# Thirteen residual additions moved from VectorE to ScalarE and an adding DMA

## The chip, the cores and the metric

The kernel runs on one core of a Trainium2 chip. Five engines work side by side, each with its own queue that is served in order: TensorE (PE in the profile; PEld is its weight load), VectorE (DVE), ScalarE (ACT), GpSimd (POOL) and SyncE (SP), whose queue issues the DMAs of this kernel. The metric is the device time of one execution in microseconds.

## The reference

Two layers, each of a Fourier mixing block and a linear attention block, on x with 2048 rows and 640 columns:

```
x = x + Real(DFT_seq(DFT_hidden(layernorm(x))))      # block A
x = x + attention(layernorm(x)) @ wo                 # block B
x = x + Real(DFT_seq(DFT_hidden(layernorm(x))))      # block A
x = x + attention(layernorm(x)) @ wo                 # block B, the last pass is its second half
...
q, k, v = x @ wqkv, in 32 heads of 20
phi(t)  = where(t > 0, t + 1, exp(t)) + 1e-6
num = phi(q) @ (phi(k)^T v)          # per head
den = phi(q) . sum(phi(k)) + 1e-6
out = (num / den) @ wo
```

## The kernel before, in words

The rows of x lie in SBUF as 16 tiles of 128x640 (x0 to x15 in the profile), and stay there through all four blocks. Every matmul with weights is done as three products of rounded parts: a value is split into a high part (a cast, L180 on ScalarE) and a low part (the rest, L181, on VectorE or GpSimd), and the products high-high, high-low and low-high are summed in PSUM (`product`, L242).

The last pass is `outputs` of the second attention. It goes over the tiles n = 0 to 15. Ahead of tile n, several steps are made for later tiles:

- `weigh(m)` (L567): GpSimd multiplies the tile's phi(q) with the sums of phi(k), into a temporary (t) or a slot (s);
- `weighted(m)`: VectorE sums that over each head (L583, into den), adds 1e-6 (L584), takes the reciprocal (L585) and scales phi(q) with it (L587, L593);
- the scaled tile is transposed: for most tiles by TensorE into PSUM (L193); for the tiles in QTURNS (7, 9, 10, 11, 12, 13, 15) by a copy on ScalarE in another order (L661), a DMA out to memory and one back (`turn_out`, L201, and `turn_in`, L205; turn in the profile), and a transpose within blocks on VectorE (L210);
- the transposed tile is split into its high and its low part (L180, L181); the low parts of tiles 7 and 13 are GpSimd's (QLOWS), the others are VectorE's.

Then 30 pairs of matmuls make the product with the five combined weights (M, L242) in PSUM, VectorE adds it to x (the residual, L678), and SyncE's queue stores the tile to the output (L1325). A store goes out whole, or in two halves for the tiles in HALVES; tile 15 is multiplied, added and stored in halves.

Temporaries (t) come from a pool of 12 buffers, the PSUM tiles (ps) from one of 4. A scheduler of the language sets the order on VectorE, ScalarE, GpSimd and TensorE from its own estimate of times, and `k.ahead` moves single steps forward or back in it. SyncE's queue keeps the order of the code.

A check of the inputs (the lines from L1224 on) runs beside the work; its verdict, the flag, is read by every engine at the end of the pass.

Of the kernel before, what the change touches and what calls it, by code (L numbers as in the profile page):

```python
# [8 lines left out]
F32 = mybir.dt.float32  # L9
F32R = mybir.dt.float32r  # L10
AF = mybir.ActivationFunctionType
ALU = mybir.AluOpType
# [28 lines left out]
ANORM = ((1, 2, 4, 9, 13), (1, 2, 3, 5, 7, 8, 10, 12, 14))  # L41
QTURNS = (7, 9, 10, 11, 12, 13, 15)
QLEAD = 2
LULLS = (0, 0)
WLEAD = 4
WSLOTS = (7, 8, 9, 11, 12, 13)
VERDICT = 4
QLOWS = (5, 6, 7, 8, 13)
HALVES = (0, 1)
KEEP = (1, 2)  # L50
TOTAL = (3, 0)
EARLY = (14, 14)
# [13 lines left out]
class Spared:  # L66

    def __init__(self, k, pool):
        self.k, self.nc, self.pool = k, k.nc, pool
# [28 lines left out]
class K:  # L98
    def __init__(self, tc, ctx):
        self.tc, self.nc = tc, tc.nc  # L100
        nc = self.nc
        self.n = self.layer = self.part = 0
        self.general, self.ve = False, nc.vector
        self.cst = ctx.enter_context(tc.tile_pool(name="cst", bufs=1))
        self.psp = ctx.enter_context(tc.tile_pool(name="ps", bufs=4, space=bass.MemoryType.PSUM))
        self.ident = self.cst.tile([128, 128], F32, name="ident")
        make_identity(nc, self.ident)
        self.ones = self.cst.tile([128, 128], F32, name="ones")
        nc.vector.memset(self.ones, 1.0)
        self.mhalf = self.cst.tile([128, 1], F32, name="mhalf")  # L110
        nc.vector.memset(self.mhalf, -0.5)
        self.two = self.cst.tile([128, 2], F32, name="two")
        nc.vector.tensor_scalar(self.two, self.ident[:, 0 : 65 : 64], -1.0, 2.0, op0=ALU.mult, op1=ALU.add)

# [110 lines left out]
def halves(pu):  # L225
    return pu.rearrange("p (a b) -> p a b", a=2)[:, :, :HD]


def h2(t):
    return t.rearrange("p (a b) -> p a b", a=2)  # L230


def product(nc, pu, sh, sl, wh, wl, hs=range(2), cs=None):
    n, m = len(sh), sh[0].shape[1]
    for c in range(n) if cs is None else cs:
        for s, w, first, last in (
            (sh[c], wh[c], c == 0, False),
            (sh[c], wl[c], False, False),
            (sl[c], wh[c], False, c == n - 1),
        ):  # L240
            for h in hs:
                nc.tensor.matmul(  # L242
                    pu[:m, 512 * h : 512 * h + HD], s, w[:, HD * h : HD * h + HD], start=first, stop=last
                )


class Attention:
# [239 lines left out]
    def combine(self, G, late):  # L487
# [17 lines left out]
        with k.ahead("weigh", 0):  # L505
            qd = self.weighted(0, self.weigh(0))
            t1 = None if LULLS[k.layer] else self.weigh(1)
        late[0]()
# [3 lines left out]
        for js in ((NE - 1, NE - 2), range(NE - 2)):  # L512
# [8 lines left out]
            for j in js:  # L521
# [10 lines left out]
                kv[j] = hi, lo  # L532
        if LULLS[k.layer]:
            t1 = self.weigh(1, None, lull)
# [35 lines left out]
    def weighted(self, n, t1, ps=None):  # L570

        k, nc, pq = self.k, self.k.nc, self.PQ[self.order2[n]]
        heads = lambda t: t.rearrange("p (h d) -> p h d", d=DH)
        if ps is not None:
            den, rden = ps[:, :H], ps[:, H:]
        else:
            den, rden = (  # L580
                k.sm.tile([128, H], F32, tag="sm" + n, name=k.nm(n), bufs=2) for n in ("den", "rden")
            )
        nc.vector.tensor_reduce(den, heads(t1), axis=AX.X, op=ALU.add)  # L583
        k.ve.tensor_scalar(den, den, 1e-6, None, op0=ALU.add)  # L584
        nc.vector.reciprocal(rden, den)  # L585
        chunks = t1.rearrange("p (i c) -> p i c", i=ND)
        k.ve.tensor_tensor(  # L587
            chunks[:, :, :EC].rearrange("p i (h d) -> p i h d", d=DH),
            pq[:, : EC * ND].rearrange("p (i h d) -> p i h d", i=ND, d=DH),
            rden[:, : 6 * ND].rearrange("p (i h) -> p i h", i=ND).unsqueeze(3).to_broadcast([128, ND, 6, DH]),  # L590
            op=ALU.mult,
        )
        k.ve.tensor_tensor(  # L593
            chunks[:, :, EC:].rearrange("p i (h s) -> p h i s", h=2),
            pq[:, EC * ND :].rearrange("p (h i s) -> p h i s", h=2, i=ND),
            rden[:, 6 * ND :].unsqueeze(2).unsqueeze(3).to_broadcast([128, 2, ND, 4]),
            op=ALU.mult,
        )
        return t1
# [42 lines left out]
    def outputs(self, after, between=lambda n: None):  # L642

        k, nc, X = self.k, self.k.nc, self.X
        q = self.first
        wt, t1 = {1: self.next}, self.t1
        turns, lead = (QTURNS, WLEAD) if self.saved else ((), 3)
        early = lambda m: QLEAD if m in turns else 0
        for n, i in enumerate(self.order2):
            for m in range(n + 3, n + 1 + lead + QLEAD):  # L650
                if m < NT and m not in t1 and m not in wt and m - lead - early(m) <= n:
                    t1[m] = self.weigh(m, self.slot() if m in WSLOTS else None)
            if n + 1 < NT and n + 1 not in turns:
                tp = k.transposed(wt[n + 1])
            for m in range(n + 2, n + 3 + QLEAD):
                if m in t1 and m - 2 - early(m) <= n:
                    with k.ahead("weigh", m):
                        wt[m] = self.weighted(m, t1.pop(m))
                    if m in turns:
                        mixed = self.slot()  # L660
                        k.nc.scalar.copy(  # L661
                            mixed.rearrange("p (a b i) -> p b a i", a=4, b=ND),
                            wt[m].rearrange("p (b a i) -> p b a i", a=4, b=ND),
                        )
                        wt[m] = k.turn_in(k.turn_out(mixed), self.slot())
            pu = k.psum()
            parts = [range(2)] if n + 1 < NT else [(0,), (1,)]
            pus = [pu] + [k.psum() for _ in parts[1:]]
            for pu, hs in zip(pus, parts):
                product(nc, pu, *q, [m[0] for m in self.M], [m[1] for m in self.M], hs)  # L670
            between(n)
            if n + 1 < NT:
                with k.ahead("q", n):
                    q = k.turned(wt[n + 1], n + 1 in QLOWS) if n + 1 in turns else k.split_chunks(tp)
            for pu, hs in zip(pus, parts):
                of = lambda t: t[:, hs[0] : hs[-1] + 1, :]
                with k.ahead("res", n):
                    k.ve.tensor_tensor(of(h2(X[i])), of(h2(X[i])), of(halves(pu)), op=ALU.add)  # L678
                for h in [(x, x + 1) for x in hs] if n in HALVES and self.saved else [(hs[0], hs[-1] + 1)]:
                    after(i, *h)  # L680
# [848 lines left out]
```

## Time and profile before

| | us |
|---|---|
| median of 3 runs | 750.06 (749.22 to 750.5) |
| the profiled execution | 750.05 |
| its span | 748.1 |
| TensorE busy | 726.8 (97% of the span) |
| VectorE busy | 587.5 (79%) |
| ScalarE busy | 370.6 (50%) |
| GpSimd busy | 248.8 (33%) |
| chain that ended last: TensorE, VectorE, ScalarE | 80%, 11%, 5% |
| all DMA transfers | 98.79 MB on one hardware queue |

Times in the rows are microseconds from the start of the span, unless a column is in ns. A row of the chain of waits gives start, duration and what ran. A row of busy time by stage gives a window, and then the busy microseconds of each engine with its count of instructions. In a row of instructions the bracket at the end gives the idle time before, and what ended it.

### The profile page before, as it was taken

How to read it: one execution, taken by the hardware profiler on the slowest of the kernel's cores; microseconds unless marked ns; L12 is line 12 of the kernel's file. 1: busy time of each engine (PE TensorE's matmuls, PEld its weight loads, DVE VectorE, ACT ScalarE, POOL GpSimd, SP SyncE). 2: the span in 40 equal slices, each digit the busy share in tenths (PEclk: the TensorE clock that was granted, in tenths of full speed). 3: DMA queues.
4: the chain of work that ended last, by engine and by line, in shares of the span. 5: the costliest groups of instructions: out<-in, count | busy, mean ns of one | idle time of the engine just before them, and what ended most of it. 6: DMA issues, size and time to landing. Idle time of an engine off the chain costs nothing.

```text
span 748.1 us, 12729 instructions
## 1 busy us (share of the span) xinstructions
PE 726.8 (97%) x4734; PEld 690.4 (92%) x4734; DVE 587.5 (79%) x1156; ACT 370.6 (50%) x691; POOL 248.8 (33%) x281
## 2 busy tenths in 40 slices
PE   4999999999999999999999999999999999999998
PEld 1388999999999999899986999999999999989997
DVE  7997798768968785888984756966887886689983
ACT  7745655664345543455773336566532554441220
POOL 5237942120014002567773672026000020154300
PEclk9999999999999999999999999999999999999999
DMA  9332467345565840500043222644266435002553
GB/s 328 102 90 89 130 199 259 119 140 181 187 187 184 284 145 21 155 5 1 11 136 138 70 94 78 222 145 166 57 177 189 153 114 155 23 12 72 175 155 133
DMA packets 55549, 98.79 MB, mean 132 GB/s; under 512 B 5268, under 2 KB 22935, under 8 KB 55479
## 3 DMA queue, kind: packets, MB, share of 16 engines
q1 hardware_dynamic: 55479, 97.89, 41.2%
q8 instruction: 39, 0.64, 0.3%
q14 instruction: 31, 0.25, 0.1%
HBM read 75.84 MB, written 21.63 MB: 130 GB/s over the span
## 4 chain that ended last, share of the span: by engine, by line
PE 80%; DVE 11%; ACT 5%; issue 2%; DMA 1%; POOL 1%; SPq 0%; DVEq 0%; ACTq 0%
PE ps L242 49%; PE ps L335 18%; PE ps L1150 4%; PE ps L1096 4%; PE ps L517 2%; PE ps L193 1%; PE ps L1055 1%; DVE t L181 1%; DVE w L181 1%; ACT t L879 1%; DVE ps L583 1%; DVE x L609 1%; ACT t L880 1%; ACT ab L916 1%; DVE t L587 1%
## 5 line engine op out<-in xcount | busy, mean ns | idle before, releaser
L242 PE MATMUL ps<-w,t 128*128 128x320 f32 x2880 | 432.6, 310 | 0.5 <-DVE w L181 0.2
L242 PEld LDWEIGHTS ps<-w,t 128*128 128x128 f32 x2880 | 422.9, 188 | 2.2 <-DVE t L181 0.7
L335 PE MATMUL ps<-t,t 128*128 128x256 f32 (+1 forms) x640 | 139.9, 309 | 0.0
L1224 DVE CUSTOM_DVE_ANT_0 junk<-ck,ck 128x688 bf16<-128x688 f32 (+5 forms) x138 | 103.6, 751 | 6.4 <-DMA ck<-in_ck 4.7
L335 PEld LDWEIGHTS ps<-t,t 128*128 128x128 f32 x640 | 106.9, 188 | 0.0
L335 PE MATMUL ps<-w,t 128*128 128x384 f32 (+1 forms) x320 | 98.6, 310 | 0.6 <-DVE w L181 0.6
L367 ACT ACTIVATE t<-ps 128x640 f32<-128x640 f32 x64 | 45.1, 704 | 95.8 <-PE ps L242 95.7
L180 ACT CAST t<-t 128x640 fp32r<-128x640 f32 x62 | 45.2, 728 | 71.2 <-DVE t L210 41.1
L567 POOL TENSOR_TENSOR t<-pq,t 128x640 f32<-128x640 f32 x26 | 42.1, 1626 | 105.6 <-ACT t L485 76.9
L404 POOL TENSOR_TENSOR t<-t,s 128x640 f32<-128x640 f32 x16 | 28.7, 1792 | 129.4 <-DVE s L370 122.6
L335 PEld LDWEIGHTS ps<-w,t 128*128 128x128 f32 x320 | 60.2, 188 | 1.1 <-DVE w L181 0.9
L181 DVE TENSOR_TENSOR t<-t,t 128x640 fp32r<-128x640 f32 x52 | 43.3, 833 | 18.9 <-ACT t L180 11.1
L1096 PE MATMUL ps<-t,u 128*128 128x322 f32 x306 | 48.1, 315 | 1.3 <-DVE t L181 1.3
L1096 PEld LDWEIGHTS ps<-t,u 128*128 128x128 f32 x306 | 45.9, 189 | 2.5 <-issue 1.6
L369 ACT ACTIVATE t<-t 128x640 f32<-128x640 f32 x64 | 47.5, 742 | 0.0
L370 DVE SCALAR_TENSOR_TENSOR pq<-t,pq 128x640 f32<-128x640 f32 x32 | 27.7, 864 | 23.8 <-ACT t L369 23.8
L370 DVE SCALAR_TENSOR_TENSOR s<-t,s 128x640 f32<-128x640 f32 x32 | 26.9, 841 | 21.6 <-ACT t L369 21.4
L180 ACT CAST t<-ps 128x640 fp32r<-128x640 f32 (+1 forms) x36 | 24.9, 690 | 38.1 <-PE ps L193 34.9
L181 POOL TENSOR_TENSOR t<-t,t 128x640 fp32r<-128x640 f32 x10 | 16.3, 1634 | 74.5 <-ACT t L180 74.5
L180 ACT CAST t<-s 128x640 fp32r<-128x640 f32 x32 | 23.3, 728 | 29.7 <-DVE t L181 17.3
L1150 PE MATMUL ps<-cw,ab 128*128 128x512 f32 x80 | 35.6, 595 | 1.2 <-ACT ab L916 0.7
L181 DVE TENSOR_TENSOR t<-ps,t 128x640 fp32r<-128x640 f32 (+1 forms) x36 | 29.3, 815 | 8.2 <-ACT t L180 8.2
(196 smaller groups left out, 987.2 us busy)
## 6 DMA issues: line engine op xcount, KB each, us to landing
ck<-in_ck SPq DMA_DIRECT2D x48, 346.0 KB
ck<-in_ck SPq DMA_DIRECT2D x48, 344.0 KB
turn<-t SPq DMA_DIRECT2D x23, 320.0 KB
save<-w SPq DMA_DIRECT2D x20, 320.0 KB
w<-save SPq DMA_DIRECT2D x20, 320.0 KB
z<-turn SPq DMA_DIRECT2D x19, 320.0 KB
x<-in_x SPq DMA_DIRECT2D x16, 320.0 KB
out<-x SPq DMA_DIRECT2D x13, 320.0 KB
```

The lines of the kernel that those rows point to most:

```text
L180: self.nc.scalar.copy(hi, src)
L181: return self.engine(pool).tensor_tensor(lo, src, hi.bitcast(F32), op=ALU.subtract)
L242: nc.tensor.matmul(pu[:m, 512 * h : 512 * h + HD], s, w[:, HD * h : HD * h + HD], start=first, stop=last)
L335: nc.tensor.matmul(self.place(G, c, part), x[:, 128 * c : 128 * c + 128], p[:, f : f + n], start=start and i == 0, stop=stop and i == 2, s ...
L367: nc.scalar.activation(h2(e), halves(pu), AF.Relu, scale=-1.0)
L369: nc.scalar.activation(e, e, AF.Exp, scale=-1.0)
L370: k.ve.scalar_tensor_tensor(out, e, 1e-6, out, op0=ALU.add, op1=ALU.add)
L404: k.engine(n not in PKSUMS[k.layer]).tensor_tensor(pksum, pksum, pk, op=ALU.add)
L567: k.behind(k.nc.gpsimd.tensor_tensor(t1, self.PQ[self.order2[n]], self.zb, op=ALU.mult), lull)
L1096: self.k.nc.tensor.matmul(po[:, o : o + 322], s[:, f : f + 128], w[:, x, :], start=start, stop=stop)
L1150: self.k.nc.tensor.matmul(self.sum(j), T.out["o", q][:, 128 * j : 128 * j + 128], self.C[2, g], start=n == 0, stop=n == 3)
L1224: i = nc.vector.tensor_tensor_reduce(k.junk[:, : a.shape[1]], b, a, 1.0, 0.0, op0, op1, o)
```

## The change

For tiles 1 to 13 of the last pass, VectorE's residual is replaced: ScalarE copies the product from PSUM to a temporary y, and a DMA issued from GpSimd's queue adds y to the tile of x in SBUF. The tile is stored one step later (ALAG), and the store waits for that DMA. Tiles 0, 14 and 15 keep VectorE's residual. Tile 14 is now the one that is stored in halves, beside 0 and 15; tile 1 is stored whole. In the last pass the addition of 1e-6 to den of tiles 2 to 15 is an activation of ScalarE, whose constant is a new tile `tiny` that GpSimd fills at the start.

```
+ADDED = (1, 2, 3, 4, 5, 6, 7, 8, 9, 10, 11, 12, 13)
+ALAG = 1
+SHIFTED = tuple(range(2, 16))
-HALVES = (0, 1)
+HALVES = (0, 14)
...
+        self.tiny = self.cst.tile([128, 1], F32, name="tiny")
+        nc.gpsimd.memset(self.tiny, 1e-6)
...
-        k.ve.tensor_scalar(den, den, 1e-6, None, op0=ALU.add)
+        if k.part == 3 and n_ in SHIFTED and not k.general:
+            nc.scalar.activation(den, den, AF.Identity, bias=k.tiny)
+        else:
+            k.ve.tensor_scalar(den, den, 1e-6, None, op0=ALU.add)
...
+            if n - ALAG in landed:
+                after(landed.pop(n - ALAG), 0, 2)
+            if self.saved and n in ADDED:
+                y = k.temp()
+                with k.ahead("res", n):
+                    nc.scalar.copy(h2(y), halves(pu))
+                    nc.gpsimd.dma_start(X[i], y, accum_op=ALU.add)
+                landed[n] = i
+                continue
```

The scheduler sets the order anew around these instructions. Three places follow; the lines of the changed program stand higher by 5 to 17 (L567 is L572, L181 is L186, L201 and L205 are L206 and L210, L1325 is L1342), and buffer numbers differ.

GpSimd's queue, from the weighing of tile 5 (t_1314) to the low part of tile 7 (t_1372 before, t_1377 now). Before:

```order
L567 TENSOR_TENSOR t_1314_7573<-pq_1262_7287,t_1234_7216 128x640
L567 TENSOR_TENSOR t_1322_7628<-pq_1279_7386,t_1234_7216 128x640
L567 TENSOR_TENSOR t_1342_7747<-pq_972_5525,t_1234_7216 128x640
L567 TENSOR_TENSOR s_1341_7745<-pq_879_4979,t_1234_7216 128x640
L567 TENSOR_TENSOR s_1349_7814<-pq_900_5097,t_1234_7216 128x640
L567 TENSOR_TENSOR s_1360_7876<-pq_925_5226,t_1234_7216 128x640
L181 TENSOR_TENSOR t_1372_7941<-t_1370_7939,t_1371_7940 128x640
```

And now:

```order
L572 TENSOR_TENSOR t_1314_7575<-pq_1262_7289,t_1234_7218 128x640
L572 TENSOR_TENSOR t_1323_7630<-pq_1279_7388,t_1234_7218 128x640
L689 DMA x1_100<-t_1322_7627 128x640
L689 DMA x2_102<-t_1330_7681 128x640
L572 TENSOR_TENSOR s_1344_7751<-pq_879_4981,t_1234_7218 128x640
L572 TENSOR_TENSOR s_1353_7822<-pq_900_5099,t_1234_7218 128x640
L572 TENSOR_TENSOR t_1345_7753<-pq_972_5527,t_1234_7218 128x640
L689 DMA x3_104<-t_1343_7748 128x640
L689 DMA x4_106<-t_1352_7819 128x640
L572 TENSOR_TENSOR s_1365_7886<-pq_925_5228,t_1234_7218 128x640
L689 DMA x5_108<-t_1364_7883 128x640
L186 TENSOR_TENSOR t_1377_7951<-t_1375_7949,t_1376_7950 128x640
```

Five adding DMAs now stand between the weighings and ahead of tile 7's low part.

VectorE's queue, where the last weight split (w_1304) and the first dens of the pass (den_1309 of tile 2, den_1317 of tile 3) stand. Before:

```order
L583 TENSOR_REDUCE den_1309_7528<-t_1305_7516 128x32
L181 TENSOR_TENSOR w_1298_7485<-ps_1296_7477,w_1297_7484 120x640
L181 TENSOR_TENSOR w_1301_7498<-ps_1299_7490,w_1300_7497 120x640
L584 TENSOR_SCALAR den_1309_7528<-den_1309_7528 128x32
L583 TENSOR_REDUCE den_1317_7583<-t_1306_7518 128x32
L181 TENSOR_TENSOR w_1304_7511<-ps_1302_7503,w_1303_7510 120x640
```

And now:

```order
L588 TENSOR_REDUCE den_1309_7530<-t_1305_7518 128x32
L186 TENSOR_TENSOR w_1298_7487<-ps_1296_7479,w_1297_7486 120x640
L186 TENSOR_TENSOR w_1301_7500<-ps_1299_7492,w_1300_7499 120x640
L588 TENSOR_REDUCE den_1317_7585<-t_1306_7520 128x32
L186 TENSOR_TENSOR w_1304_7513<-ps_1302_7505,w_1303_7512 120x640
```

The addition of 1e-6 is gone from between them; the rest kept its order.

SyncE's queue at the end of the pass, from the turn of tile 15 on. Before:

```order
L1325 DMA out_0<-x9_114 128x640
L1325 DMA out_0<-x10_116 128x640
L201 DMA turn_1410_8161<-s_1409_8159 128x4x160
L205 DMA s_1411_8163<-turn_1410_8161 128x640
L1325 DMA out_0<-x11_118 128x640
L1325 DMA out_0<-x12_120 128x640
L1325 DMA out_0<-x13_122 128x640
L1325 DMA out_0<-x14_128 128x640
L1325 DMA out_0<-x15_130 128x320 x2
```

And now:

```order
L1342 DMA out_0<-x8_114 128x640
L1342 DMA out_0<-x9_116 128x640
L206 DMA turn_1420_8181<-s_1419_8179 128x4x160
L210 DMA s_1421_8183<-turn_1420_8181 128x640
L1342 DMA out_0<-x10_118 128x640
L1342 DMA out_0<-x11_120 128x640
L1342 DMA out_0<-x12_122 128x640
L1342 DMA out_0<-x13_124 128x640
L1342 DMA out_0<-x14_130 128x320 x2
L1342 DMA out_0<-x15_132 128x320 x2
```

Each store of an added tile moved behind the turn of one step later, so that the turn of tile 15 now stands behind the store of tile 9 and not of tile 10.

More of the change, by code (lines that the diff above doesn't have):

```diff
@@ L570, in weighted @@
     def weighted(self, n, t1, ps=None):
-        k, nc, pq = self.k, self.k.nc, self.PQ[self.order2[n]]
+        k, nc, pq, n_ = self.k, self.k.nc, self.PQ[self.order2[n]], n
         heads = lambda t: t.rearrange("p (h d) -> p h d", d=DH)
@@ L645, in outputs @@
         q = self.first
-        wt, t1 = {1: self.next}, self.t1
+        wt, t1, landed = {1: self.next}, self.t1, {}
         turns, lead = (QTURNS, WLEAD) if self.saved else ((), 3)
```

## The prediction

> **What bounds the kernel now.** I read the busy time by stage first, then the chain of waits over the last pass, then the groups of instructions of that pass, and last the rows of GpSimd and of the DMA queue. The busy time (engines in the order PE, PEld, DVE, ACT, POOL; then granted clock, DMA share, GB/s):
>
> ```profile
> span 748.1 us, 12729 instructions
> 660.00:680.00 20.00, 18.24 (x124) 16.88 (x123) 17.57 (x32) 8.28 (x13) 11.52 (x8) 1.00 0.11 28
> 680.00:700.00 20.00, 20.00 (x143) 19.92 (x142) 19.96 (x38) 4.63 (x8) 5.70 (x4) 1.00 0.35 117
> 700.00:720.00 20.00, 20.00 (x137) 19.55 (x136) 19.87 (x35) 5.39 (x8) 6.73 (x4) 1.00 0.51 167
> 720.00:735.00 15.00, 15.00 (x105) 14.99 (x104) 8.80 (x14) 2.78 (x4) 1.57 (x1) 1.00 0.55 173
> 735.00:748.10 13.10, 9.41 (x65) 9.14 (x63) 4.65 (x6) 0.73 (x1) 0.00 (x0) 0.94 0.29 107
> ```
>
> From 680 to 720 us two engines are full at once: TensorE (40.0 of 40) and VectorE (39.8 of 40). Which of them sets the time is read from the chain:
>
> ```profile
> 667.43 0.72 DVE den L583
> 668.16 1.46 DVE w L181 x2
> 669.62 0.09 DVE den L584
> 669.71 0.72 DVE den L583
> 670.43 0.73 DVE w L181
> ...
> 673.12 0.83 PE ps L242 x4
> 673.95 0.55 PE ps L193 x5
> 674.50 4.39 PE ps L242 x30
> 678.88 0.55 PE ps L193 x5
> 679.43 4.39 PE ps L242 x30
> 683.82 0.55 PE ps L193 x5
> ...
> 688.77 0.55 PE ps L193 x5
> ...
> 693.73 0.55 PE ps L193 x5
> ...
> 698.67 0.11 PE ps L1245
> ...
> 703.99 26.68 PE ps L242 x180
> 730.66 0.55 PE ps L193 x5
> 731.21 13.21 PE ps L242 x90
> 744.42 0.02 issue
> 744.44 0.49 DVE x L678
> ```
>
> From 673.12 to 744.42 us every step of the chain is a matmul. A product of one tile (30 pairs, L242) takes 4.39 us, and six of them without a transpose between take 26.68 / 6 = 4.45. VectorE is full, but it is never late: nothing of it ends a wait of TensorE in these 71.3 us. So the 13 residuals that leave VectorE lie beside matmuls, and their time is not on the path.
>
> **The change part by part.** The groups of this pass from 673 us on (count | busy us, mean ns | idle time before):
>
> ```profile
> L678 DVE TENSOR_TENSOR x<-x,ps 128x640 f32<-128x640 f32 (+1 forms) x17 | 13.0, 770 | 6.5 <-PE ps L242 6.5
> L584 DVE TENSOR_SCALAR den<-den 128x32 f32<-128x32 f32 x12 | 4.7, 402 | 0.0
> L180 ACT CAST t<-ps 128x640 fp32r<-128x640 f32 x7 | 4.9, 694 | 19.2 <-PE ps L193 19.2
> L661 ACT COPY s<-s 128x640 f32<-128x640 f32 x5 | 3.6, 727 | 9.2 <-DVE s L593 9.2
> L181 DVE TENSOR_TENSOR t<-ps,t 128x640 fp32r<-128x640 f32 x7 | 5.7, 814 | 0.5 <-ACT t L180 0.5
> L567 POOL TENSOR_TENSOR t<-pq,t 128x640 f32<-128x640 f32 x4 | 6.3, 1570 | 10.9 <-issue 6.7 <-DVE t L593 4.2
> L181 POOL TENSOR_TENSOR t<-t,t 128x640 fp32r<-128x640 f32 x2 | 3.1, 1568 | 33.3 <-ACT t L180 33.3
> ```
>
> *VectorE* loses 13 x 0.77 = 10.0 us of residuals and 14 additions of 1e-6 (4.7 us for twelve), about 15 of 71 us. On the path this counts once: L584 stands for 0.09 us ahead of the last weight split (670.43), whose rows TensorE waits for at 673.12. Gain 0.09 us.
>
> *ScalarE* gains 13 copies out of PSUM; its nearest operation, the cast of the same shape from PSUM, takes 0.69, so 9.0 us, and 14 additions of 128x32 with no row of their own: between 0.1 (a short VectorE operation) and 0.69 each, taken as 0.2, so 2.8. It was busy 4.63 to 8.28 us in 20, so it has room. But its queue is in order: each copy waits for the end of a product, and the next tile's cast stands behind it. After the end of product n come the copy (0.69), mostly one reordering copy or addition (0.7), the cast (0.7) and VectorE's low part (0.8): 2.9 us, and the result is due 4.4 + 0.6 us after that end, when product n + 2 reaches its third pair. Spare 2.1 us, so nothing. VectorE's reciprocals now wait for ScalarE's additions behind the same copies; in the order they stand behind a low part that needs the same point of ScalarE's queue, so they take nothing more.
>
> *GpSimd* gains 13 DMA issues, each behind the copy of its tile, with weighing products (L567) and two low parts (L181) queued behind. The rows before:
>
> ```profile
> 680.54 5.16 POOL L567 TENSOR_TENSOR s<-pq,t 128x640 f32<-128x640 f32 x3
> 700.66 1.57 POOL L181 TENSOR_TENSOR t<-t,t 128x640 fp32r<-128x640 f32 x1 [14.96 <-ACT t L180]
> 702.18 2.09 POOL L567 TENSOR_TENSOR s<-pq,t 128x640 f32<-128x640 f32 x1
> 704.23 1.57 POOL L567 TENSOR_TENSOR t<-pq,t 128x640 f32<-128x640 f32 x1
> ```
>
> No row shows what such an issue holds GpSimd for; call it d. The nearest below is an issue of SyncE's queue, 0.34 us (row further down), the nearest above GpSimd's longest single operation here, 2.09. I take 1.6, its usual pass over 128 rows. Then: tile 1 from 679.6 (product end 678.88 + 0.7), tile 2 from 684.5 to 686.1, three weighings to 690.9, tile 3 to 692.5, tile 4 from 694.4 to 696.0, a weighing to 697.6, tile 5 from 699.4 to 701.0, and tile 7's low part from 701.0 to 702.6. Product 7 starts at 703.99 and wants it 0.6 us later: 2.0 us spare. Both ends of d cost nothing; with a larger d the issues queue up, and the low part ends at 692.5 + 4d, which passes 704.6 at d = 3.0. At tile 13 the sum is 726.9 + d + 1.6 against 731.8, d = 3.3.
>
> *The transfers.* Rows of the DMA queue, and of VectorE where it waited for one:
>
> ```profile
> 707.92 0.34 SPq L1325 DMA_DIRECT2D out<-x  x1
> 708.35 0.39 SPq L201 DMA_DIRECT2D turn<-s  x1
> ...
> 719.36 0.39 SPq L201 DMA_DIRECT2D turn<-s  x1
> 722.59 0.32 SPq L205 DMA_DIRECT2D s<-turn  x1
> ...
> 725.91 1.36 DVE L210 STREAM_TRANSPOSE t<-s 128x640 f32<-128x640 f32 x1 [1.55 <-DMA s<-turn]
> 738.73 6.56 SPq L1325 DMA_DIRECT2D out<-x  x4
> ```
>
> A plain 320 KB transfer takes 3.2 us from issue to landing (719.36 to 722.59). The adding one, from GpSimd's issue to landing (A), reads its destination too: from below 3.2, from above two transfers one after the other, 6.5. I take 4.5, nearer to the one, since from the row of 735 to 748.1 us the engines move 1.40 MB in 0.29 x 13.1 = 3.8 us, so a further pass of 320 KB is only 0.9.
> The page "DMA: Bandwidth & Descriptors" of the Trainium skill (Anatomy of one DMA) fits 2.0 us + bytes/436e3 to a transfer of GpSimd's queue; worked out as an estimate that is 2.75 us for 320 KB, and the sum would be the same by it, as it lies below every point at which A begins to cost.
>
> Who waits for A: SyncE's stores, and behind them the turning transfers of later tiles. Tile 13's turn stands behind the store of tile 7. Product 7 ends at 703.99 + 4.45 = 708.4; copy to 709.1, landing 713.6, turn out and in 6.5 more, 720.1, against 725.91 before, since the store of tile 8 no longer stands there. The others keep 5 us or more as well. Temporaries come free when an addition has landed; the tightest (ScalarE's copies of tiles 3 and 4, about 5 us after the landing of 1 and 2) allow A = 9. Cost 0. The DMA engines had 0.35 x 20 + 0.51 x 20 + 0.55 x 15 = 25.5 of 55 us busy from 680 to 735; eleven additions may take 2.7 us each before they are full, three plain passes.
>
> *The end.* Product 13 ends at 731.21 + 13.21 / 3 = 735.6, its copy at 736.3, the addition lands at 740.8, two microseconds later than its store went out before (738.73), and it is stored then; tile 14 in two issues follows by 741.6, tile 15's halves at 742.7 and 744.93 as before. SyncE's issues stand 0.43 us apart (707.92, 708.35), so the last is late only when tile 13 lands after 744.93 - 4 x 0.43 = 743.2, A = 6.9. Cost 0; for stores closer together at the end allow up to 0.3. The transpose of tile 14 moves by 28 matmuls into product 12 and stays the same 0.55 us.
>
> **Sum:** 0.09 gained, 0 to 0.3 lost at the end. The profiled execution took 750.05 us, its span 748.1 and 1.95 around it, and the median of the runs shown is 750.06. I forecast 749.9, no change that can be told: 0.2% is 1.5 us, about what a measurement of this kernel can tell.
>
> **The rivals.**
> *GpSimd's issue is long (slower).* Place: tile 7's low part behind the additions of 1 to 5; it decides from d = 3.0. At d = 4 the low part ends at 692.5 + 16 = 708.5, 3.9 us late: 754. Against it: 3.0 is above every single GpSimd operation of the pass. For it: VectorE and GpSimd hold each other up. L584 took 402 ns on average here but 0.09 in the chain, and the GpSimd product at 702.18 took 2.09 where its neighbour took 1.57. A VectorE operation that holds GpSimd out lasts up to 1.36 (the transpose at 725.91), so d = 1.6 + 1.36 = 2.96 if each issue meets one, and two such would make 4.3, 5.1 us late, 755.
> The Trainium skill's "SBUF — State Buffer" (A bandwidth-pool intuition) has the same trap: GpSimd cannot write its descriptors while VectorE uses the shared ports, and a transfer of 0.62 us took 3.1; by that figure as an estimate of d the low part would end at 704.9, 0.3 us late. The trace shows such blocking between operations, but no issue.
> *The additions are slow (slower).* If they take the DMA engines more than three passes, these are full and landings pile up; at the end each microsecond of A above 6.9 is one of time. A = 10 gives 750 + 3.1 = 753. Against it: A = 6.5 already charges two full transfers. For it: no adding transfer is in any row.
> *VectorE was the bound after all (faster).* If it were, 15 us less work would show. What is there to win is the wait in the first product (669 to 673.12, some 0.6 us beyond a product's 4.4) and 6 x 0.05 in the later ones: 749.1 at best, within 0.2%; for more the matmuls' spacing itself would have to shorten.
>
> **Chances.** No change that can be told 0.54; long issues 0.23 and slow additions 0.18, both slower by over 0.2%; faster by over 0.2% 0.05. Range: the forecast with its own bounds is 749.1 to 750.3, from which the low end is rounded down to 749.0; since the slower cases hold 0.41, it reaches to 755.5, past 753, 754 and 755, and leaves about 0.05 below and 0.13 above. Alone the likeliest case would have 749.0 to 750.6.
>
> **What would show it.** Right: TensorE's chain unbroken from 673 to 744, VectorE with some 15 us less from 680 to 735, GpSimd's low part of tile 7 done before 704, the store of tile 13 issued by 741. Wrong: a matmul (L242) that waits for GpSimd at product 7 or 13, SyncE's stores waiting over 5 us for an addition, DMA shares near 1, or the last store issued after 745.3. The forecast falls if d is above 3 us or A above 7.

## The result and the profile after

The changed kernel takes 752.65 us (median of 14 runs, 751.15 to 757.78) against 750.0 us of the kernel before beside it (14 runs); the medians differ by 2.65 us. The ratio, taken over all these runs, is 1.0041, 95% interval 1.0029 to 1.0052, or 3.1 us slower. The profiled execution of the changed kernel took 752.29 us, its span 750.2.

The busy time by stage of the changed kernel (PE, PEld, DVE, ACT, POOL; then granted clock, DMA share, GB/s):

```profile
span 750.2 us, 12769 instructions
660.00:680.00 20.00, 18.25 (x125) 17.49 (x125) 18.87 (x29) 9.56 (x18) 10.85 (x7) 1.00 0.11 27
680.00:700.00 20.00, 18.35 (x130) 18.01 (x129) 18.44 (x26) 7.49 (x15) 8.80 (x7) 1.00 0.67 165
700.00:720.00 20.00, 20.00 (x139) 19.79 (x139) 18.28 (x27) 9.52 (x17) 11.69 (x9) 1.00 0.85 214
720.00:735.00 15.00, 14.14 (x95) 13.48 (x94) 6.56 (x9) 4.76 (x8) 4.09 (x4) 1.00 0.90 225
```

TensorE, without a gap here before, loses 1.65 us between 680 and 700 and 0.86 between 720 and 735. The DMA share has gone from 0.35, 0.51 and 0.55 to 0.67, 0.85 and 0.90. TensorE's rows at the two gaps, with what ended each:

```profile
697.22 0.83 PE L247 MATMUL ps<-w,t 128*128 128x320 f32 x4
699.71 4.07 PE L247 MATMUL ps<-w,t 128*128 128x320 f32 x26 [1.65 <-DVE t L186]
...
727.61 4.89 PE L247 MATMUL ps<-w,t 128*128 128x320 f32 x30
733.36 12.85 PE L247 MATMUL ps<-w,t 128*128 128x320 f32 x86 [0.86 <-POOL t L186]
```

Product 6 waits after 4 of its 30 for VectorE's low part, and product 13 after 4 of its 30 for GpSimd's. Executions differ by a microsecond or two in what lies ahead of the last pass, so I measure from the start of the pass's first product (668.94 before, 667.59 now). To the start of product 7 it is 34.80 us before (668.94 to 703.74) and 36.74 now (667.59 to 704.33), 1.94 more. From there to the last matmul's end it is 40.66 (703.74 to 744.40) and 41.88 (704.33 to 746.21), 1.22 more. From there to the end of the span it is 3.70 and 3.99, 0.29 more. The sum is 3.45, and the runs show 3.1.

**The first gap.** GpSimd, VectorE and ScalarE of the changed kernel, in turn:

```profile
683.88 0.86 POOL L689 DMA_DIRECT2D x<-t  x1 [4.16 <-ACT t L688]
684.46 3.40 POOL L572 TENSOR_TENSOR s<-pq,t 128x640 f32<-128x640 f32 x2
687.51 1.86 POOL L572 TENSOR_TENSOR t<-pq,t 128x640 f32<-128x640 f32 x1
...
685.32 4.70 DVE L595 TENSOR_TENSOR s<-pq,rden 128x600 f32<-128x600 f32 x1
696.63 2.08 DVE L601 TENSOR_TENSOR t<-pq,rden 128x40 f32<-128x40 f32 x1
698.90 0.75 DVE L186 TENSOR_TENSOR t<-ps,t 128x640 fp32r<-128x640 f32 x1
...
690.22 0.73 ACT L669 COPY s<-s 128x640 f32<-128x640 f32 x1 [5.83 <-DVE s L601]
690.85 0.69 ACT L688 COPY t<-ps 128x640 f32<-128x640 f32 x1
691.44 0.69 ACT L185 CAST t<-ps 128x640 fp32r<-128x640 f32 x1
```

VectorE's scaling of phi(q) (L595), 0.71 to 0.78 us in this pass where GpSimd runs nothing beside it, lasts 4.70 us here: it starts inside the first of three weighing products that stand directly behind the adding DMA of tile 2, and ends 0.65 us after the last of them (689.37). A second operation of VectorE (L601, 0.19 without a GpSimd operation beside it) takes 2.08 at 696.63, behind the adding DMA of tile 4 and one weighing product (696.20 to 698.65). Behind the first, ScalarE's queue stands too: its reordering copy waits 5.83 us, and the copy of product 3 out of PSUM and the cast of tile 5 wait behind it, so that tile 5's low part starts at 692.17. Tile 6's low part is then the end of a backlog on VectorE: it is done at 699.65, and product 6, whose first four matmuls ended at 698.05, goes on at 699.71.

In the kernel before, four weighing products also ran in a row (679.02 to 685.70), but VectorE's rows there show no operation held for more than one of them:

```profile
679.93 1.30 DVE L587 TENSOR_TENSOR t<-pq,rden 128x600 f32<-128x600 f32 x1
681.16 1.56 DVE L593 TENSOR_TENSOR t<-pq,rden 128x40 f32<-128x40 f32 x1
684.10 1.64 DVE L584 TENSOR_SCALAR den<-den 128x32 f32<-128x32 f32 x2
```

**The second gap.** SyncE's queue of the changed kernel, with the turns of tiles 11, 12 and 13, and GpSimd's low part of tile 13:

```profile
706.76 0.39 SPq L206 DMA_DIRECT2D turn<-s  x1
713.84 0.32 SPq L210 DMA_DIRECT2D s<-turn  x1
...
714.73 0.40 SPq L206 DMA_DIRECT2D turn<-s  x1
720.06 0.33 SPq L210 DMA_DIRECT2D s<-turn  x1
720.44 1.04 SPq L1342 DMA_DIRECT2D out<-x  x1
721.57 0.52 SPq L206 DMA_DIRECT2D turn<-s  x1
726.02 0.32 SPq L210 DMA_DIRECT2D s<-turn  x1
...
731.73 1.58 POOL L186 TENSOR_TENSOR t<-t,t 128x640 fp32r<-128x640 f32 x1 [3.23 <-issue]
```

The turns out of tiles 11, 12 and 13 take 7.1, 5.3 and 4.4 us here (706.76 to 713.84, 714.73 to 720.06, 721.57 to 726.02), and all five from 701 on take 4.4 to 7.1; the seven of the kernel before took 2.6 to 3.4. SyncE waits for each before it issues the turn in, so tile 13's turn leaves at 721.57, and tile 13's low part is done 0.05 us before product 13 goes on at 733.36. The groups of the adding DMA, its queue over the whole kernel, and issue to landing (the last number of the last row):

```profile
L689 POOL DMA_DIRECT2D x<-t x13 | 11.5, 885 | 33.5 <-ACT t L688 30.0 <-ACT den L590 3.5
q0 software_dynamic: 1872, 4.26, 3.2%
x<-t POOLq DMA_DIRECT2D x13, 320.0 KB, 4.6
```

One adding DMA holds GpSimd 0.885 us, lands after 4.6 (median) and keeps all 16 DMA engines busy for 3.2% x 750.2 / 13 = 1.85 us.

### The profile page after: what moved, and what is told of

Its sections match the earlier page's. It is cut to its first block, busy times and chain, and to the rows that moved or that the text cites. A ratio compares the mean times of both kernels' runs of the same rounds, so it can differ in the third digit from the quotient of the medians.

```text
span 750.2 us, 12769 instructions
## 1 busy us (share of the span) xinstructions
PE 727.8 (97%) x4734; PEld 690.6 (92%) x4734; DVE 580.7 (77%) x1129; ACT 382.0 (51%) x718; POOL 259.7 (35%) x295
## 3 DMA queue, kind: packets, MB, share of 16 engines
q0 software_dynamic: 1872, 4.26, 3.2%
## 4 chain that ended last, share of the span: by engine, by line
PE 76%; DVE 10%; ACT 5%; DMA 4%; issue 2%; POOL 1%; SPq 1%; DVEq 0%; ACTq 0%
PE ps L247 42%; PE ps L340 18%; PE ps L1113 6%; PE ps L1167 4%; DMA turn<-s 3%; PE ps L1072 3%; DVE t L186 2%; PE ps L522 2%; DVE t L595 1%; PE ps L198 1%; DVE w L186 1%; ACT t L896 1%; DVE ps L588 1%; DVE x L617 1%; ACT t L897 1%
## 5 line engine op out<-in xcount | busy, mean ns | idle before, releaser
L572 POOL TENSOR_TENSOR t<-pq,t 128x640 f32<-128x640 f32 x26 | 43.8, 1692 | 100.4 <-ACT t L490 77.6
L186 DVE TENSOR_TENSOR t<-t,t 128x640 fp32r<-128x640 f32 x52 | 43.9, 844 | 22.1 <-ACT t L185 14.4
L186 DVE TENSOR_TENSOR t<-ps,t 128x640 fp32r<-128x640 f32 (+1 forms) x36 | 29.2, 811 | 10.5 <-ACT t L185 9.6
L160 POOL TENSOR_TENSOR kept<-ve,mhalf 128x1 f32<-128x1 f32 x32 | 21.7, 695 | 40.5 <-DVE ve L159 39.3
```

The lines of the kernel that those rows point to most:

```text
L186: return self.engine(pool).tensor_tensor(lo, src, hi.bitcast(F32), op=ALU.subtract)
L572: k.behind(k.nc.gpsimd.tensor_tensor(t1, self.PQ[self.order2[n]], self.zb, op=ALU.mult), lull)
```

## The experiments

Two theories first. H: GpSimd's weighing products, bunched behind the adding DMAs, hold VectorE out, and product 6 waits. L: the additions slow the turning transfers, and product 13 and the last store wait. Each kernel was timed in five rounds beside the kernel before (750.24 to 750.75 us there).

**One twentieth of the bytes.**

```
-                    nc.gpsimd.dma_start(X[i], y, accum_op=ALU.add)
+                    nc.gpsimd.dma_start(X[i][:, :32], y[:, :32], accum_op=ALU.add)
```

> Each adding DMA carries only the first 32 of 640 columns (the other 608 columns of these residuals are left out), so GpSimd's queue, the copies and all waits stay and the load on the DMA engines goes. Two theories of the 3.1 us: H, that GpSimd's weighings in a row behind the DMA of tile 2 hold VectorE out (one L595 of 4.70 us) and product 6 waits 1.65 us; L, that the additions load the DMA engines (1.8 us each), turns take 4.4 to 7.0 us instead of 3.2, and product 13 waits 1.3 us and the last store 0.3. Both: 751.7, product 6 still waits. H alone: 752.4. L alone: 750.0, and no wait at product 6.

Measured 752.34, ratio 1.0026 (1.0016 to 1.0036), 2.0 us. VectorE's held row and TensorE's rows of this kernel have the first gap whole and the second gone (the last row runs from product 12 to the end):

```profile
686.39 4.71 DVE L595 TENSOR_TENSOR s<-pq,rden 128x600 f32<-128x600 f32 x1
700.77 4.07 PE L247 MATMUL ps<-w,t 128*128 128x320 f32 x26 [1.66 <-DVE t L186]
728.68 17.26 PE L247 MATMUL ps<-w,t 128*128 128x320 f32 x116
```

So the first gap does not hang on the bytes that are added, and the second does; the 2.0 us that stay are about the first gap's 1.94. SyncE's stores wait for additions here as long as in the changed kernel (16.2 us in all from 674 to 730, against 15.9). The turns of tiles 10 and 11 take 2.7 and 3.5 us in place of 4.6 and 7.1, but those of tiles 12 and 13 still take 5.3 and 4.4.

**A plain DMA in place of the adding one.**

```
-                    nc.gpsimd.dma_start(X[i], y, accum_op=ALU.add)
+                    nc.gpsimd.dma_start(X[i], y)
```

> The same DMA without the addition (x of tiles 1 to 13 is overwritten by the product, the sum with x is left out); the order on every engine is the same. L: one pass instead of two, so 0.9 us of the DMA engines in place of 1.8 for each, turns of about 4 us, product 13 hardly waits: 751.7. H alone: 752.6, as the changed kernel.

Measured 751.37, ratio 1.0013 (1.0003 to 1.0023), 1.0 us. VectorE's L595 is held for 4.39 us and the L601 behind it for 1.76, 0.63 us less in all than in the changed kernel; product 6 waits 1.06, 0.59 less, and product 13 not at all. The same 4.26 MB take 1.5% of the span here, not 3.2%, in the row of the DMA queue:

```profile
q0 software_dynamic: 1040, 4.26, 1.5%
```

That is 1.5% x 749.3 / 13 = 0.86 us of all engines for each plain DMA, and an issue holds GpSimd 0.54 to 0.58 us (the first 0.82). Adding costs twice the transfer time and 0.3 us of GpSimd per issue.

**The first six tiles alone, the last seven alone.**

```
-ADDED = (1, 2, 3, 4, 5, 6, 7, 8, 9, 10, 11, 12, 13)
+ADDED = (1, 2, 3, 4, 5, 6)          # the one
+ADDED = (7, 8, 9, 10, 11, 12, 13)   # the other
```

> Only tiles 1 to 6 by the adding DMA, 7 to 13 by VectorE as before. H: the burst behind tile 2 stays, product 6 waits 1.65 us, nothing later: 751.7. L: the turns of tiles 11 to 15 come free again and nothing waits at product 13: with L alone 750.0.

> Only tiles 7 to 13 by the adding DMA, 1 to 6 by VectorE as before; GpSimd's weighings run early again. H: no long VectorE instruction and no wait at product 6, so 750.0 with H alone. L: the later turns are as slow as in the changed kernel, product 13 waits 1.3 us and the last store 0.3: 751.5.

Measured 753.29, ratio 1.0034 (1.0022 to 1.0047), 2.6 us, for the first six; 751.13, ratio 1.0007 (0.9998 to 1.0015), 0.5 us, for the last seven. With the first six, L595 is held 4.72 us, product 6 waits 1.68, and product 8 waits 0.89 more, behind a further VectorE operation, held 2.28 us by an issue and the weighing product behind it. H had priced the first six at less: it had left out the second place. With the last seven the DMA share from 720 to 735 us is the highest so far, and yet TensorE is without a gap there, in the busy time by stage:

```profile
720.00:735.00 15.00, 15.00 (x106) 15.00 (x105) 7.69 (x11) 4.98 (x8) 4.33 (x5) 1.00 0.97 254
```

So most of the loss comes from tiles 1 to 6, and load of the DMA engines as such does not make product 13 wait.

**Only the other half of the change**, the 1e-6 by ScalarE and tile 14 stored in halves.

```
-ADDED = (1, 2, 3, 4, 5, 6, 7, 8, 9, 10, 11, 12, 13)
+ADDED = ()
```

> Only the other half of the change: ScalarE adds the 1e-6, and tile 14 is the one that is taken in two halves; the residuals stay VectorE's additions out of PSUM and no adding DMA is issued. H and L both put the whole loss on the adding DMAs and the order round them: 750.0 to 750.3, the same as before, with no wait of TensorE between the products. Rival S (VectorE's reciprocals wait for ScalarE's additions of 0.32 us behind other work in ScalarE's queue, and this makes the low parts late): 751 to 752 with a wait of a product for VectorE's low part.

Measured 749.94, ratio 0.9995 (0.9985 to 1.0004): no change, and no wait of a product. The whole loss belongs to the adding DMAs and the order round them.

**Weighing products earlier, stores later, and both.**

```
-WLEAD = 4
+WLEAD = 6       # first and third kernel
-ALAG = 1
+ALAG = 2        # second and third kernel
```

> All 13 adding DMAs stay, but GpSimd's weighing products are written out two tiles earlier (WLEAD 6 for 4), so that most of them stand ahead of the first adding DMA instead of behind the first two. H (weighings held behind the issues come in a row and hold VectorE out): VectorE's chunk product (L595) no longer takes over 4 us near 685, product 6 does not wait for VectorE, and the time falls by 1.7 to 2 us to 750.8 to 751.2; what stays is product 13's wait of 1.3 us and the later last store. Rival (VectorE's low part of tile 6 is late for another reason, such as ScalarE's copies ahead of its cast): the wait of 1.65 us before product 6 stays and so does the time, 752.6.

> Each tile's store on SyncE's queue is written out one tile later (ALAG 2 for 1), so that it stands behind one more turning transfer and its addition has 4.4 us more to land. L as a matter of the queue (SyncE's stores stand waiting for additions and hold up the turning transfers behind them): tile 13's turn is issued several us before 721, product 13 does not wait, and 1.3 us come back: 751.5, the wait before product 6 as it is. L as a matter of load (the turning transfers themselves are slow because the adding ones share the DMA engines): the turns still take 4.4 to 7 us, product 13 still waits, 752.6. Either could lose up to 0.5 us at the end, where a store more is left behind the last product.

> Both repairs at once, all 13 adding DMAs kept: weighings two tiles earlier, stores one tile later. If H and the queue reading of L are the whole loss, both waits are gone and the time is 749.9 to 750.4, no different from the kernel before; if L is load, product 13's wait stays, 751.2. If it came below 749.5, the 15 us taken from VectorE would be worth something after all, which the unbroken TensorE chain of the kernel before speaks against.

Weighings earlier: 752.33, ratio 1.0031 (1.0019 to 1.0043), 2.3 us. Product 6 no longer waits, as H had it, but the time hardly falls. More weighing products now stand at the start of the pass, in a row up to 676.2, and hold VectorE there, one at a time (an L601 of 1.54 us at 672.67). The second product starts 6.07 us after the first (668.77 to 674.84; 5.31 before, 668.94 to 674.25), and product 13 still waits; TensorE's rows:

```profile
674.35 0.74 PE L198 MATMUL ps<-ident,t 128*128 128x128 f32 x5 [0.56 <-DVE t L601]
733.20 12.90 PE L247 MATMUL ps<-w,t 128*128 128x320 f32 x86 [0.77 <-POOL t L186]
```

Stores later: 754.87, ratio 1.0063 (1.0050 to 1.0077), 4.7 us. Product 13 no longer waits, as the queue reading had it; but the order on GpSimd moved by one weighing product, a further L595 is held (1.67 us, 693.77), and product 6 waits 2.83 us in place of 1.65. Both: 750.75, ratio 1.0008 (0.9999 to 1.0017), 0.6 us; no product waits after the second. Of the kernel with both, the turn of tile 13 on SyncE's queue, and the busy time of the two stages round it:

```profile
715.01 0.38 SPq L206 DMA_DIRECT2D turn<-s  x1
721.09 0.33 SPq L210 DMA_DIRECT2D s<-turn  x1
700.00:720.00 20.00, 20.00 (x139) 19.79 (x139) 13.34 (x24) 8.71 (x15) 8.96 (x8) 1.00 0.91 230
720.00:735.00 15.00, 15.00 (x105) 15.00 (x104) 5.52 (x6) 3.93 (x6) 4.18 (x4) 1.00 0.95 252
```

The DMA engines are fuller than in the changed kernel (0.91 and 0.95 against 0.85 and 0.90) and the turn takes 6.1 us, longer than there. But it starts 46.2 us after the first product (668.81 to 715.01), where it started 54.0 after it (667.59 to 721.57). So product 13's wait needs both: slow turns, and stores ahead of them in SyncE's queue that wait for additions. In the changed kernel these are the stores of tiles 1 to 4, ahead of the turns of 7, 9 and 10; from 701 to the turn of tile 13 none waits for one, and the queue moves on only as turns land. That the additions slow the turns is shown for tiles 10 and 11 alone; what makes those of 12 and 13 slow in the kernel with 32 columns too, these runs do not separate.

**One issue, and the same without an issue.** All holds of VectorE through more than one product so far stood directly behind a DMA issue of GpSimd; where four products ran in a row without one, in the kernel before, with the last seven and with the other half alone, VectorE got its turn. Theory G makes that the cause. Both kernels have the residuals on VectorE; STRAY is (1,), and the added statements are shown on lines of their own.

```
+        self.stray = self.cst.tile([128, 32], F32, name="stray")
...
                     k.ve.tensor_tensor(of(h2(X[i])), of(h2(X[i])), of(halves(pu)), op=ALU.add)
+                    self.saved and n in STRAY and nc.gpsimd.dma_start(k.stray, X[i][:, :32])      # the one
+                    self.saved and n in STRAY and nc.gpsimd.tensor_copy(k.stray, X[i][:, :32])    # the other
```

> No adding DMA at all: the residuals stay VectorE's additions (as with the moved 1e-6 alone), but behind tile 1's residual stands one plain 128x32 DMA of GpSimd's queue (16 KB, from x to a tile that nobody reads), so that four weighing products stand directly behind one issue that waited for tile 1, near 684. Theory G (behind a DMA issue GpSimd's operations run one after the other and VectorE's chunk product gets no turn between them): one VectorE operation on two SBUF operands (L595 or L601) lasts over 4 us there, and a product some 15 us later may wait 1 to 2 us: 751 to 752. Rival B (it is the late, dense run of weighings as such, and VectorE gets its turn after each): no VectorE operation lasts over 2.2 us, 750.0 to 750.5.

> The same kernel with GpSimd copying the 128x32 itself in place of the DMA issue: same wait for tile 1's residual, same four weighing products behind it, no issue. G: VectorE gets a turn after each weighing product, no VectorE operation on two SBUF operands lasts over 2.2 us, 750.0 to 750.5. If holding the weighing products back and running them close together is enough (B's opposite: any operation of GpSimd ahead of them does it), one lasts over 4 us as behind the issue and the time is that of the kernel with the issue.

With the issue: 757.22, ratio 1.0093 (1.0078 to 1.0109), 7.0 us for one transfer of 16 KB. Its rows of GpSimd, VectorE and TensorE:

```profile
680.85 0.82 POOL L695 DMA_DIRECT2D stray<-x  x1 [5.92 <-DVE x L695]
681.70 1.58 POOL L572 TENSOR_TENSOR t<-pq,t 128x640 f32<-128x640 f32 x1
683.22 4.52 POOL L572 TENSOR_TENSOR s<-pq,t 128x640 f32<-128x640 f32 x3
681.15 6.65 DVE L601 TENSOR_TENSOR t<-pq,rden 128x40 f32<-128x40 f32 x1
689.32 6.70 PE L247 MATMUL ps<-w,t 128*128 128x320 f32 x26 [4.56 <-DVE t L186]
```

Without it: 751.11, ratio 1.0010 (1.0001 to 1.0019), 0.75 us, of which a wait of 0.47 stands before one product for VectorE's late residual. VectorE's queue has the same order; the rows of GpSimd and VectorE:

```profile
680.12 0.69 POOL L695 COPY stray<-x 128x32 f32<-128x32 f32 x1 [5.68 <-DVE x L695]
680.78 1.58 POOL L572 TENSOR_TENSOR t<-pq,t 128x640 f32<-128x640 f32 x1
682.31 5.16 POOL L572 TENSOR_TENSOR s<-pq,t 128x640 f32<-128x640 f32 x3
682.72 1.79 DVE L595 TENSOR_TENSOR s<-pq,rden 128x600 f32<-128x600 f32 x1
684.43 1.56 DVE L601 TENSOR_TENSOR s<-pq,rden 128x40 f32<-128x40 f32 x1
```

G holds. Behind the issue an operation of 0.19 us lasted 6.65, from the issue through all four weighing products, which ran without a gap (6.0 us for four). Behind the copy the last three took 5.16 us, 0.64 more than behind the issue, because VectorE had its turns in between. G had priced the issue at 1 to 2 us, at a product some 15 us later; VectorE was held through all four products, product 3 waited for it right there, and TensorE was slow after the wait (below).

**Tiles 3 to 13 alone, stores one tile later.**

```
-ADDED = (1, 2, 3, 4, 5, 6, 7, 8, 9, 10, 11, 12, 13)
+ADDED = (3, 4, 5, 6, 7, 8, 9, 10, 11, 12, 13)
-ALAG = 1
+ALAG = 2
```

> The adding DMA for tiles 3 to 13 alone, each store one tile later. GpSimd's weighing products are then not held by tiles 1 and 2 (no wait of product 6), and SyncE's turns do not stand behind the additions (no wait of product 13). H and the queue reading of L: TensorE unbroken from the second product on, 750.3 to 750.8, of which 0.3 is the later end. If the loss came with every adding DMA alike (eleven of thirteen stay), 752.2. If G alone counts: two weighing products stand behind tile 3's issue, near 693, hold VectorE for 2.9 us there and cost a product up to 1 us: 751.5.

Measured 752.87, ratio 1.0031 (1.0019 to 1.0043), 2.3 us. All readings missed the place. Products 6 and 13 do not wait for a low part. But three weighing products now stand behind the issue of tile 3 (691.98 to 696.88), VectorE has nothing to do until the first is there (1.62 us idle), an L601 is then held for 1.91 us behind the issue of tile 5 and one product (701.65), and the backlog makes product 7 wait. TensorE's row names the row of the input check, which VectorE has ready at 707.50; GpSimd's low part of tile 7 (705.65, 1.71 us) was done 0.14 us earlier:

```profile
707.64 22.36 PE L247 MATMUL ps<-w,t 128*128 128x320 f32 x150 [1.16 <-DVE ckrow L1269]
```

**GpSimd adds itself.**

```
-                    nc.gpsimd.dma_start(X[i], y, accum_op=ALU.add)
+                    nc.gpsimd.tensor_tensor(X[i], X[i], y, op=ALU.add)
```

> The change as it is, order and waits included, but GpSimd adds ScalarE's copy to x itself (128x640, some 1.6 us by its other products) in place of each adding DMA: no issue and no further load of the DMA engines. G: VectorE gets its turn after each GpSimd operation, nothing of it lasts over 2.5 us near 685, and product 6 waits at most 0.5; L: the turns take about 3 us again and product 13 does not wait for them. Time 750.0 to 751.0. Rival H without G (three weighings held behind tile 2 and run in a row are enough): VectorE held out over 4 us and product 6 waits 1.6 as in the changed kernel, 752. Rival W (13 x 1.6 us of GpSimd work more: VectorE's operations on two SBUF operands meet GpSimd far oftener, GpSimd's two low parts come late): 751.5 to 753 with waits of other products.

Measured 753.8, ratio 1.0035 (1.0021 to 1.0048), 2.6 us: rival W. Nothing on VectorE that two SBUF operands feed lasts over 1.8 us, though three weighing products run in a row again (688.46 to 693.63), and product 13 does not wait: neither cause is at work. But each addition takes GpSimd 1.55 us or more ahead of its weighing products and low parts, and products 6 and 7 wait for low parts, product 6 for one of VectorE, product 7 for one of GpSimd; that the additions make them late is argued, not shown apart. With no adding DMA at all the turns of tiles 10 and 11 take 2.6 and 2.5 us, and those of 12 and 13 again 4.8 and 4.4. TensorE's rows:

```profile
701.21 4.07 PE L247 MATMUL ps<-w,t 128*128 128x320 f32 x26 [1.06 <-DVE t L186]
708.36 22.25 PE L247 MATMUL ps<-w,t 128*128 128x320 f32 x150 [0.94 <-POOL t L186]
```

The profiles carry these times. The table has the time from the first product of the last pass to the end of the span, less the 79.16 us of the kernel before (668.94 to 748.1), beside the ratio.

| kernel | first product | span | more than before | by the ratio |
|---|---|---|---|---|
| the change | 667.59 | 750.2 | 3.45 | 3.1 |
| 32 columns | 668.67 | 750.0 | 2.2 | 2.0 |
| plain DMA | 668.86 | 749.3 | 1.3 | 1.0 |
| first six | 668.78 | 751.1 | 3.2 | 2.6 |
| last seven | 669.44 | 749.2 | 0.6 | 0.5 |
| other half alone | 671.36 | 750.4 | -0.1 | -0.4 |
| weighings earlier | 668.77 | 750.5 | 2.6 | 2.3 |
| stores later | 668.06 | 751.3 | 4.1 | 4.7 |
| both | 668.81 | 748.8 | 0.8 | 0.6 |
| one issue | 668.73 | 755.2 | 7.3 | 7.0 |
| a copy for it | 668.25 | 748.0 | 0.6 | 0.75 |
| tiles 3 to 13, later | 670.23 | 751.6 | 2.2 | 2.3 |
| GpSimd adds | 669.70 | 751.9 | 3.0 | 2.6 |

None is measurably faster than the kernel before.

## Why the prediction was right or wrong

The forecast of no change was wrong: the time is 2.65 us above the median of the kernel before beside it. That it lies in the stated range is luck: the range reached so far up for long issues and slow additions, and neither happened as told; the likeliest case alone had 749.0 to 750.6. The step that failed first is the one on VectorE, and the one on tile 13's turn failed beside it.

- **"VectorE is full, but it is never late."** True of the kernel before, and carried over to one in which GpSimd's order was new. The step on GpSimd placed three weighing products from 686.1 to 690.9, about where they ran (684.5 to 689.4, in a pass that began 1.35 us earlier); what they do to VectorE there was not asked. They held it for 4.70 us and again for 2.08, where 0.77 and 0.19 were its work, or 5.8 us more together, against a spare of 2.1 us that the step on ScalarE had worked out for the low parts without any hold. Cost 1.9 us in place of 0.
- **The cause of that**: the step on d asked what an issue holds GpSimd for, and what is late on GpSimd. Nothing in it asked who is held out by what follows the issue. The pair with and without one issue shows that this is the larger price.
- **d = 1.6 us.** Measured 0.885; the end of it that decides, 3.0, was not reached, and the rival of long issues did not happen. It named VectorE and GpSimd holding each other up, in the wrong direction: VectorE was held.
- **A = 4.5 us.** Measured 4.6 (3.6 to 6.9, and 4.6 for tile 13 at the end), and 1.85 us of the DMA engines, within the three plain passes of 0.86 that the step allowed. The rival of slow additions did not happen either as told. The further pass that the step put at 0.9 us cost the DMA engines 1.0 (1.85 against 0.86); the landing took 1.8 us more than that of the plain DMA (2.8).
- **Tile 13's turn.** Foretold for 713.6, from a product's end and plain transfers, which is 44.7 us after the first product; it was issued 54.0 after it, at 721.57. The step priced each turn at 3.2 us, where 4.4 to 7.1 were measured, and did not add up SyncE's queue, in which every turn waits for the one before and for stores that wait for additions. Such turns and the stores between take longer than a product's 4.4 us, so the queue fell behind from tile to tile. Cost 1.2 us in place of 0; in the kernels where only the slow turns or only the waiting stores were left, it was hidden. The wait at product 13 for GpSimd was among the signs of being wrong; the dearer wait of product 6 for VectorE was not.
- **ScalarE.** Copies 0.69 us as foretold, additions 0.32 in place of 0.2; its queue carried the hold of VectorE on to tile 5's cast. The step counted the reordering copy there at 0.7 us, and not the 5.83 us that it waits for VectorE.
- **The gain of 0.09** at the last weight split is not seen: from the first to the second product it is 5.31 us before and 5.33 now (667.59 to 672.92).
- **The end.** 0.29 us, inside the 0 to 0.3 allowed.
- **VectorE not the bound.** Right: with its residuals gone, nothing became faster. Its busy time fell by 6.8 us (587.5 to 580.7) and not by 15; a held operation counts as busy, and the two above alone hold 5.8 us of that.

## What to carry to other kernels

When work is moved to GpSimd's queue, ask which operations of GpSimd will stand directly behind each DMA issue, and which operation of VectorE on two SBUF operands falls into that run: it can be held for the whole of it, whatever the transfer's size. Price a transfer that waits its turn in a queue at the load that the change brings, and add the queue up step by step against the rate of the loop. Work taken from a busy engine that ends no wait on the path is worth nothing, and the order that the move upsets is its price.

## What the runs showed of the hardware

- An adding DMA of 320 KB within SBUF kept the 16 DMA engines busy for 1.85 us and held GpSimd 0.885 us; the plain one of the same bytes took 0.86 and 0.54 to 0.58 (the first 0.82).
- Behind a DMA issue, GpSimd's products on SBUF operands ran one after the other, and VectorE's operation on two SBUF operands waited for all of them: 4.4 to 4.7 us for three (in five kernels), 2.94 for two (in two), 6.65 for four. Behind a copy, an addition or nothing, it waited for one at a time. VectorE's reductions, reciprocals and low parts out of PSUM kept their usual 0.8, 0.34 and 0.8 us beside such products. The Trainium skill's "SBUF — State Buffer" (Who interferes with whom) has the lock behind this: a VectorE instruction with two SBUF inputs and a GpSimd instruction that reads SBUF exclude each other for a whole instruction. The runs agree for the operations with two; that the lock can be lost several times in a row behind an issue goes beyond it. Why it is so inside GpSimd, no run here shows. VectorE's addition of 1e-6 (L584) has one SBUF operand and was held as well, in the kernel before: 1.59 us at 704.25, beside a product, where it takes 0.10 to 0.20 with none.
- After a wait of TensorE of 4.56 us, its granted clock was 0.50, then 0.64, then 1.00 again, and 26 matmuls took 6.70 us where they take 4.07. Waits of up to 2.83 us left it at 4.07. The busy time by stage of the kernel with the one issue, in short stages:

```profile
689.00:693.00 4.00, 3.68 (x14) 3.69 (x15) 4.00 (x10) 1.57 (x3) 0.00 (x0) 0.50 0.00 0
693.00:696.00 3.00, 3.00 (x16) 2.99 (x16) 1.62 (x4) 0.00 (x0) 0.00 (x0) 0.64 0.65 218
696.00:700.00 4.00, 4.00 (x31) 4.00 (x29) 3.36 (x5) 1.95 (x4) 0.00 (x0) 1.00 0.52 168
```

  The wait of 4.56 and the slow stretch of 6.70 - 4.07 = 2.63 make 7.2 us, beside the 7.0 that this kernel lost. The Trainium skill's "TensorE: Matmul & The Clock Gate" (Part 1: The HAM clock gate) has half the clock after about 3.4 us without work, which agrees with both sides of these numbers.
